# Windowed attention in front of an MLP: blocks of 128 keys by 64 queries of two heads, with block-diagonal queries in place of block-diagonal keys, another order of the transposed copies, and V shifted on the chip

## The chip, the cores and the metric

The kernel runs on one core of one Trainium2 chip. The metric is the device time in microseconds (us) of one execution, given as the median of several. The profiles are of single executions, and their span (first to last instruction) is some 2 us shorter than the time of the same run. TensorE is called PE below, its weight loads PEld, VectorE DVE, ScalarE ACT and GpSimd POOL, as the profile does.

A run is called slow when it is over 1.5% above the fastest of the same kernel.

## The reference

```python
# q, k, v: (8 batches, 8 heads, 576, 64) float32;  w_in (512, 2048), w_out (2048, 512)
scores = q @ k.T / 8                          # per batch and head
mask   = (rel >= 0) & (rel < 64)              # rel = query position - key position
attn   = softmax(where(mask, scores, -1e9))
x      = (attn @ v), heads side by side       # 4608 tokens x 512
h      = x @ w_in
out    = (h - tanh(h)) @ w_out                # 4608 x 512 float32
```

A query sees itself and the 63 keys before it. So 64 neighbouring queries need 127 keys, and 64 neighbouring keys serve 127 queries.

## The kernel before

Both kernels weave the attention of one pair of heads (a *cycle*) into four steps of the MLP. A step is one hp product of four matmuls, tanh and a subtraction, and four matmuls of yp for the chunk of 512 tokens before. There are nine chunks of 16 steps. In the profile's names, `tp` are the transposed queries and keys in PSUM, `qt` and `kt` (or `ktb`) their copies in SBUF, `sp` the scores, `pt` their exponentials, `ov` the product PV, `rc` and `xs` the normalisation, `tpx` and `xT` the transposed output, `th` the tanh, `gT` the subtraction and `ysb` the copy of yp out of PSUM. These are the parts that the change touches; the MLP is the same in both.

```python
kTb  = [const.tile([128, S, 2], BF16) ...]        # keys: column 2t+h holds head h's 64 channels, zero elsewhere
qT   = [const.tile([128, S + 64], BF16) ...]      # queries of both heads, one above the other
vaug = [const.tile([128, NP, NJ, 130], BF16) ...] # partition 2p+i: key p of head i; a ones column per head

def load_v(b):                                    # 128-byte pieces into every second partition
    for i in range(2):
        nc.gpsimd.dma_start(out=vaug[b % NV][i::2, :, :, 65 * i:65 * i + 64]..., in_=v[...])

def tr(g, which):                                 # rows -> channels on partitions
    ...                                           # 6 transposes of 96 rows into PSUM: tp[channel, e, p]; position = 6p + e
    if which == "q":
        nc.scalar.activation(qT[g % NR][:, 0:S].rearrange("c (p e) -> c e p", e=E6), tp, ACT.Copy)
    else:
        for i in range(2):
            nc.vector.tensor_copy(
                kt[64 * i:64 * i + 64, :, i].rearrange("c (p e) -> c e p", e=E6),
                tp[64 * i:64 * i + 64])

def scores(g, grp):                               # 3 matmuls: 64 keys of two heads x 128 queries, then exp into PT
    ...
def masking(g):                                   # PT *= mask, on VectorE
    ...
def pv(g, t0, t1):                                # up to 3 matmuls per 128 queries, added up in PSUM; then 1/sum on VectorE
    ...

    # the schedule of pair g; "early" is after hp of a step, "late" is after yp
    at(early, a, tr, g, "q");          at(late, a, tr, g, "k")
    at(early, a + 1, scores, g, 0);    at(early, a + 1, scores, g, 1);  at(late, a + 1, scores, g, 2)
    at(early, a + 2, masking, g)
    at(late, a + 2, pv, g, 0, 3);      at(late, a + 3, pv, g, 3, 5)
```

The PSUM tile holds e outermost and p innermost, and the SBUF tile wants position 6p + e. The kernel before walks along p. So it reads PSUM densely and writes one 2-byte element every 12 bytes (queries) or every 24 bytes (keys, where two heads alternate).

The softmax here doesn't subtract the row's maximum and nothing guards it: scores larger than these inputs give would overflow.

## Time and profile before

| | before |
|---|---|
| time, median of 4 runs | 642.86 us (642.23 to 643.35) |
| span of the profiled run, granted clock | 641.7 us, 0.837 |
| PE busy, DVE busy | 63%, 56% |
| one cycle (one pair, four steps) | 17.0 us; 20.8 where a batch's output is transposed |

The view is the table of stretches of the kernel before: start, chunk 0, the long stage and the plain MLP at the end. Its columns are the stretch, its length, busy time and count of PE, PEld, DVE, ACT and POOL, the granted clock, the share of the DMA engines and GB/s.

```profile
0.00:71.80 71.80, 19.95 (x177) 16.72 (x178) 45.68 (x54) 17.49 (x20) 30.61 (x45) 1.00 1.22 171
71.80:144.00 72.20, 41.04 (x223) 21.87 (x221) 41.56 (x50) 22.59 (x33) 8.61 (x10) 0.66 0.19 20
144.00:553.50 409.50, 264.92 (x1619) 135.89 (x1619) 240.45 (x281) 140.12 (x206) 41.45 (x48) 0.81 0.25 49
553.50:641.70 88.20, 79.88 (x387) 36.23 (x385) 28.51 (x47) 30.23 (x51) 0.00 (x0) 0.98 0.11 42
```

The long stage is two thirds of the time, with PE busy for 65% of it at 0.81 of the clock. (The trace's clock record of this kernel begins 81 us after the start of the span, and a mean counts what lies before it as full clock. So the 1.00 of the first row is no measurement, and the 0.66 of the second is a little too high: the first hp matmuls of chunk 0, before 81 us, follow each other every 427 ns, against 216 where the record says full clock.)

### The profile page before, as it was taken

The numbers are of one execution on the slowest core, as the hardware profiler recorded it, in microseconds if no ns is written. First come the engines' busy times: TensorE is split into PE (matmuls) and PEld (weight loads), VectorE is DVE, ScalarE is ACT, GpSimd is POOL, SyncE is SP. The second block draws the span as 40 slices with busy tenths as digits, with TensorE's granted clock in tenths as the row PEclk, the third lists the DMA queues.
The fourth block names the chain that finished last, engine by engine and source line by source line (L and its number), as shares of the span: only waits on it lengthen the run. The fifth ranks groups of instructions, "written<-read, shape, count | busy, mean of one in ns | idle before, by whom it ended". The sixth has DMA issues, their size and how long they took to land.

```text
span 641.7 us, 6133 instructions
## 1 busy us (share of the span) xinstructions
PE 405.8 (63%) x2400; PEld 210.7 (33%) x2400; DVE 356.2 (56%) x431; ACT 210.4 (33%) x309; POOL 80.7 (13%) x103
## 2 busy tenths in 40 slices
PE   0145555556667666656667766656666766699996
PEld 0134222233334333333333333333333333344442
DVE  3875556566654556566664555656665555544330
ACT  2142133333333233333333333333333333334431
POOL 3912100040103110031103110031111100000000
PEclk9999966668888777778888777777889777799999
DMA  9998900060118211161119111161111100000101
GB/s 198 177 199 113 129 1 0 1 38 0 54 53 89 56 53 55 53 37 55 53 54 90 54 54 53 54 41 50 54 54 54 53 17 17 16 34 33 51 33 66
DMA packets 59964, 37.62 MB, mean 59 GB/s; under 512 B 38944, under 2 KB 55328, under 8 KB 59936
## 3 DMA queue, kind: packets, MB, share of 16 engines
q0 software_dynamic: 41440, 8.91, 17.6%
q1 hardware_dynamic: 18496, 28.32, 15.6%
q8 instruction: 19, 0.31, 0.2%
q14 instruction: 9, 0.07, 0.0%
HBM read 36.70 MB, written 9.44 MB: 72 GB/s over the span
## 4 chain that ended last, share of the span: by engine, by line
PE 42%; DVE 24%; issue 6%; ACT 5%; POOL 1%; DMA 1%; SPq 0%; POOLq 0%; ACTq 0%
DVE ktb L157 18%; PE yp L226 17%; PE hp L212 16%; PE sp L165 4%; PE ov L185 3%; DVE gT L218 3%; ACT th L215 2%; DVE pt L171 2%; PE tp L151 2%; ACT qt L153 2%; ACT ysb L231 1%; PE tpx L196 1%; DMA qf<-in_q_dram 1%; POOL qb L77 1%; DVE xT L202 0%
## 5 line engine op out<-in xcount | busy, mean ns | idle before, releaser
L218 DVE TENSOR_TENSOR gT<-hp,th 128x512 bf16<-128x512 f32 x144 | 99.6, 692 | 189.4 <-ACT th L215 188.6
L212 PE MATMUL hp<-xT,w_in_sb 128*128 128x512 bf16 x576 | 179.9, 443 | 0.1
L157 DVE COPY ktb<-tp 64x576 bf16<-64x576 bf16 x64 | 171.7, 2684 | 13.1 <-PE tp L151 11.6
L226 PE MATMUL yp<-w_out_sb,gT 128*128 128x512 bf16 x576 | 167.5, 422 | 2.8 <-ACT ysb L231 2.8
L215 ACT ACTIVATE th<-hp 128x512 f32<-128x512 f32 x144 | 89.6, 622 | 192.6 <-PE hp L212 192.6
L165 PE MATMUL sp<-qt,ktb 128*128 128x128 bf16 x288 | 42.9, 309 | 164.5 <-DVE ktb L157 163.5
L167 ACT ACTIVATE pt<-sp 128x384 bf16<-128x384 f32 x96 | 44.0, 493 | 195.9 <-PE sp L165 195.9
L165 PEld LDWEIGHTS <-ktb 128*128 128x128 bf16 x288 | 30.0, 140 | 187.7 <-DVE ktb L157 176.0
L226 PEld LDWEIGHTS <-gT 128*128 128x128 bf16 x576 | 60.7, 109 | 75.3 <-issue 30.8
L212 PEld LDWEIGHTS <-w_in_sb 128*128 128x128 bf16 x576 | 58.7, 111 | 53.5 <-issue 20.7
L153 ACT ACTIVATE qt<-tp 128x576 bf16<-128x576 bf16 x32 | 66.9, 2089 | 21.2 <-PE tp L151 21.2
L185 PE MATMUL ov<-vaug,pt 128*128 128x130 bf16 x416 | 40.3, 244 | 40.8 <-DVE pt L171 37.1
L77 POOL CAST qb<-qf 96x768 bf16<-96x768 f32 x32 | 26.6, 831 | 207.5 <-DMA qf<-in_q_dram 192.9
L185 PEld LDWEIGHTS <-pt 128*128 128x128 bf16 x416 | 30.8, 109 | 65.4 <-DVE pt L171 52.5
L89 POOL DMA_DIRECT2D vaug<-in_v_dram x14 | 16.2, 1162 | 206.7 <-PE ov L185 206.7
L191 DVE TENSOR_TENSOR xs<-ov,rc 128x384 bf16<-128x384 f32 x64 | 31.4, 491 | 2.2
L189 DVE RECIPROCAL rc<-ov 128x6 f32<-128x6 f32 x64 | 11.8, 185 | 29.6 <-PE ov L185 29.6
L231 ACT ACTIVATE ysb<-yp 128x512 f32<-128x512 f32 x36 | 21.4, 593 | 17.5 <-PE yp L226 17.5
L77 POOL CAST kb<-kf 96x768 bf16<-96x768 f32 x32 | 26.5, 829 | 0.9 <-POOL qb L77 0.3
L202 DVE COPY xT<-tpx 128x512 bf16<-128x512 bf16 (+1 forms) x44 | 15.2, 369 | 19.2 <-PE tpx L196 19.2
L171 DVE TENSOR_TENSOR pt<-pt,mask 128x1152 bf16<-128x1152 bf16 x32 | 24.0, 749 | 0.2
L151 PE MATMUL tp<-ident,qb 96*128 96x96 bf16 x192 | 15.2, 222 | 14.0 <-POOL qb L77 7.4
(26 smaller groups left out, 95.9 us busy)
## 6 DMA issues: line engine op xcount, KB each, us to landing
qf<-in_q_dram SPq DMA_DIRECT2D x32, 288.0 KB, 3.4
kf<-in_k_dram SPq DMA_DIRECT2D x32, 288.0 KB, 3.8
out_dram<-ysb SPq DMA_DIRECT2D x36, 256.0 KB, 2.1
vaug<-in_v_dram POOLq DMA_DIRECT2D x14, 288.0 KB, 7.2
w_in_sb<-in_moe_w_in_dram POOLq DMA_DIRECT2D x4, 512.0 KB, 10.0
w_out_sb<-in_moe_w_out_dram POOLq DMA_DIRECT2D x4, 512.0 KB, 22.0
vaug<-in_v_dram POOLq DMA_DIRECT2D x8, 72.0 KB, 5.5
```

The lines of the kernel that those rows point to most:

```text
L77: nc.gpsimd.tensor_copy(t.rearrange("p e h d -> p h e d"), stage.pop((g, n)).rearrange("p h (e d) -> p h e d", d=D))
L153: nc.scalar.activation(qT[g % NR][:, 0:S].rearrange("c (p e) -> c e p", e=E6), tp, ACT.Copy)
L157: nc.vector.tensor_copy(kt[64 * i:64 * i + 64, :, i].rearrange("c (p e) -> c e p", e=E6), tp[64 * i:64 * i + 64])
L165: nc.tensor.matmul(sp[:, i, :], kTb[g % NR].rearrange("c t h -> c (t h)")[:, 128 * j:128 * j + 128], qT[g % NR][:, 64 * j:64 * j + 128], s ...
L167: nc.scalar.activation(PT[g % NR][:, 3 * grp:3 * grp + 3, 0:128], sp, ACT.Exp, scale=scale)
L171: nc.vector.tensor_tensor(p, p, mask.unsqueeze(1).to_broadcast([128, NJ, 128]), ALU.mult)
L185: nc.tensor.matmul(ov[:, t - t0, :], ptf[:, c0:c0 + 128], vaug[b % NV][:, pr, j, :], start=(i == 0), stop=(i == len(parts) - 1))
L191: nc.vector.tensor_tensor(xo, ovr[:, :, :, 0:64], rc[:, 0:n].to_broadcast([128, n, 2, 64]), ALU.mult)
L212: nc.tensor.matmul(hp, w_in_sb[:, ki, m * 128:(m + 1) * 128], chunk_tile(c)[:, ki, :], start=(ki == 0), stop=(ki == 3))
L215: nc.scalar.activation(th, hp, ACT.Tanh)
L218: nc.vector.tensor_tensor(gT[c][:, m, :], hp, th, ALU.subtract)
L226: nc.tensor.matmul(yps[c, s], gT[c][:, m, s * 128:(s + 1) * 128], w_out_sb[:, m, :], start=(m == 0), stop=(m == M - 1))
```

## The change

Its intent: lay a block out as 128 keys by 64 queries of two heads. Then the keys stay plain, the queries become block-diagonal (two copies of half a tile), one PV matmul of 128 keys serves a window of 64 queries of both heads, and nothing has to be added up in PSUM. The 128 keys are the window's own 64 and the 64 before; so V stands twice in SBUF, the second time moved on by one block of 64 keys, by a transfer on the chip (`shift_v`). The copies after the transposes now walk along the written side, so that the stepping is on the PSUM side. The core of the diff:

```diff
+    vw = [const.tile([128, NP, NJ, 129], BF16, ...)]      # partitions 64-127: keys of block j; 0-63: of block j-1
+    kT = [const.tile([128, 64 + S], BF16, ...)]
+    qT = [const.tile([128, NJ, 2, 64], BF16, ...)]
+    def load_v(b, p0=0, p1=NP):
+        for i in range(2):
+            nc.gpsimd.dma_start(out=vw[b % NV][64:128, p0:p1, :, 64 * i:64 * i + 64]..., in_=v[...])
+    def shift_v(b, p0=0, p1=NP):
+        w = vw[b % NV].rearrange("p r j c -> p r (j c)")
+        nc.sync.dma_start(out=w[0:64, p0:p1, 129:], in_=w[64:128, p0:p1, :(NJ - 1) * 129])
 ...
     def tr(g, which):
 ...
-            nc.scalar.activation(qT[g % NR][:, 0:S].rearrange("c (p e) -> c e p", e=E6), tp, ACT.Copy)
+            t = tp.rearrange("c e (j a) -> c j e a", a=8)
+            o = qT[g % NR].rearrange("c j h (e a) -> c j h e a", e=E)
+            nc.scalar.activation(o[0:64, :, 0], t[0:64], ACT.Copy)
+            nc.vector.tensor_copy(o[64:128, :, 1], t[64:128])
         else:
-            for i in range(2):
-                nc.vector.tensor_copy(
-                    kt[64 * i:64 * i + 64, :, i].rearrange("c (p e) -> c e p", e=E6),
-                    tp[64 * i:64 * i + 64])
+            nc.scalar.activation(kT[g % NR][:, 64:].rearrange("c (p e) -> c p e", e=E),
+                                 tp.rearrange("c e p -> c p e"), ACT.Copy)
 ...
     def pv(g, grp):
+        for i in range(3):
+            j = 3 * grp + i
+            nc.tensor.matmul(ov[:, i, :], PT[g % NR][:, j, :], vw[b % NV][:, pr, j, :], start=True, stop=True)
+        # one reciprocal and two multiplies (one per head) for each group of three windows
 ...
-        at(late, a + 2, pv, g, 0, 3)
-        at(late, a + 3, pv, g, 3, 5)
+        at(late, a + 2, pv, g, 0)
+        at(early, a + 3, pv, g, 1)
+        at(late, a + 3, pv, g, 2)
 ...
+    at(late, -8, load_v, 1)
+    at(late, -4, shift_v, 1)
+    for i in range(4):
+        at(late, -3 + i, load_w_out, i)
```

Cut are the memsets, the mask, the casts, the transposes of the output (now half a batch at a time), and the writes of the result, which put the rows of a window back into their order.

## The prediction

> **What bounds the kernel now.** I read the page first: no engine is full (PE 63%, VectorE 56% of the 641.7 us span), so a sum of busy time does not decide. The chain that ended last does: 18% of the span lies on one VectorE line, the copy that makes the block-diagonal keys.
>
> ```profile
> PE 42%; DVE 24%; issue 6%; ACT 5%; POOL 1%; DMA 1%; SPq 0%; POOLq 0%; ACTq 0%
> ...
> L157 DVE COPY ktb<-tp 64x576 bf16<-64x576 bf16 x64 | 171.7, 2684 | 13.1 <-PE tp L151 11.6
> ...
> L165 PE MATMUL sp<-qt,ktb 128*128 128x128 bf16 x288 | 42.9, 309 | 164.5 <-DVE ktb L157 163.5
> ```
>
> The third row says what it costs: TensorE stood 163.5 us before the score matmuls, all of it for that copy. It is 32 waits of 5.1 us, one for each pair of heads. Next, the chain in order of time in the middle of the run, over one such cycle (one pair of heads and four steps of the two MLP matmuls, hp and yp):
>
> ```profile
> 311.91 0.26 PE tp L151 x6
> 312.17 0.86 PE yp L226 x4
> 313.04 0.27 PE tp L151 x6
> 313.31 0.02 issue
> 313.33 2.69 DVE ktb L157
> 316.03 0.01 issue
> 316.04 2.69 DVE ktb L157
> 318.73 0.05 issue
> 318.78 0.82 PE sp L165 x6
> 319.60 1.71 PE yp L226 x4
> 321.31 0.32 PE sp L165 x3
> 321.63 1.72 PE hp L212 x4
> ```
>
> Two copies of 2.69 us stand between the transposes of the keys and the scores, and only one hp (0.86 us) lies beside them. The cycle repeats after 17.0 us (scores at 301.79, 318.78, 335.79). And the same yp of four matmuls takes 0.86 us before the wait and 1.71 after it. The table of short stretches (time, length, busy and count of PE, PEld, VectorE, ScalarE, POOL, then the granted clock) shows why:
>
> ```profile
> 309.78:313.19 3.41, 3.41 (x31) 1.99 (x30) 1.90 (x5) 1.84 (x3) 1.49 (x2) 1.00 0.00 0
> 313.19:316.60 3.41, 0.97 (x7) 0.23 (x3) 3.34 (x3) 1.77 (x2) 0.00 (x0) 0.97 0.00 0
> 316.60:320.02 3.42, 1.24 (x8) 0.92 (x9) 2.81 (x2) 0.70 (x2) 0.00 (x0) 0.50 0.00 0
> 320.02:323.43 3.41, 3.41 (x13) 1.41 (x11) 0.00 (x0) 1.21 (x4) 0.00 (x0) 0.53 0.00 0
> ```
>
> A stretch of 3.41 us with PE busy for only 0.97 is followed by two at half clock. So each wait is paid twice: 4.6 to 5.1 us idle and some 3 us of work at half speed.
>
> The hp matmuls give the stages: start until the first hp 71.8 us; then 27 cycles until 553.5 (17.0 us each, 20.8 where a batch's output is transposed into xT); then 88.2 us of plain MLP, where hp and yp follow each other every 0.86 us, at PE's speed.
>
> **What the Trainium skill says.** "TensorE: Matmul & The Clock Gate", Part 1: the clock is halved after a window of about 3.4 us with little activity and restored after a busy one. The trace agrees: over all stretches of 3.41 us, those at full clock with 0.8 to 1.2 us of PE work were followed by half clock, those with 1.96 or more stayed; none lies between. "SBUF — State Buffer", Specifications: SBUF has 16-byte lines, and each access that goes to a new line pays. It agrees: the keys' copy writes one 2-byte element every 24 bytes and takes 2684/576 = 4.7 ns an element, ScalarE's copy of the queries (every 12 bytes) 2089/576 = 3.6; copies that write dense (xT: 419 ns for 512, 283 for 256) take 0.53 and a fixed 147. "VectorE: DVE Perf Modes", The perf-mode tier table: a bf16 copy from PSUM may do two elements a cycle, tensor_tensor from PSUM one. It agrees (0.53 above; xs: 558 ns for 384, 424 for 256, so 1.05 ns and a fixed 156). "PSUM — Partial Sum Buffer", Specifications: 8-byte lines in PSUM. No row here shows what a stepped 2-byte read from PSUM costs.
>
> **Removed.** The two key copies, 2 x 2684 ns on VectorE per pair, and the 2089 ns query copy on ScalarE. Four PV matmuls per pair (13 become 9). Start: two memsets of 2.0 us and the ones columns.
>
> **Added per pair.** Keys: one ScalarE copy, dense writes, stepped reads. From exp (384: 493 ns), tanh (512: 622) and ysb (512: 593) I take 0.66 us for 576. Queries: half on ScalarE (0.66), then half on VectorE, which in the order of instructions waits for ScalarE's half; 147 + 576 x 0.53 = 0.45 us, or 0.76 at one element a cycle. Normalisation in three groups of three windows instead of two: three reciprocals of 0.16 and six multiplies of 64x192, 156 + 192 x 1.05 = 0.36 us each; 2.6 us against 1.35. Transposes: 16 of 72 columns for 12 of 96. Other additions: the shift of V (0.5 MB per batch, sync queue) and two output DMAs for one; both hidden, nine steps ahead of use or behind the end. VectorE saves 5.4 + 1.35 - 0.45 - 2.6 = 3.7 us per pair, but the gain is the wait.
>
> **One cycle after, at full clock.** PE: 8 x 0.86 for hp and yp, 16 transposes 0.6, 9 scores 0.5, 9 PV 0.5: 8.5 us. Latencies from the trace: hp's start to tanh 1.07, tanh 0.60, gT 0.69, 0.03 to 0.06 between engines. Now I lay the four steps out, zero at hp of step A:
> - A: hp to 0.86, transposes of q to 1.16, yp to 2.02, transposes of k to 2.32. ScalarE: tanh to 1.67, q half to 2.35, k to 3.2. VectorE: gT to 2.39, q half to 2.86.
> - B: hp to 3.18; scores at 3.26, a wait of **0.1** in place of 5.1; yp and the last scores to 4.63. ScalarE: tanh to 4.0, three exps to 5.35, ysb to 5.92.
> - C: hp to 5.49; yp needs its one PSUM buffer, which ysb frees at 5.92: wait **0.5**, to 6.84. Tanh after ysb to 6.52, gT to 7.24, mask 0.75 to 7.97; PV 1 waits **1.2** (the trace before has 1.2 there too), to 8.17.
> - D: hp to 9.03; the one ov buffer is free after reciprocal and two multiplies at 9.2: wait **0.2**; yp to 10.29. Now gT of D stands first on VectorE (to 10.56), then 0.9 us of normalisation: PV 3 waits **1.2**, to 11.67.
>
> So 8.5 + 3.2 = 11.7 us. Where half a batch is transposed (every second pair) 9 transposes (0.5) and waits for two tp buffers (0.8) are added: 13.0. Mean 12.3, against 17.95 (three of 17.0, one of 20.8).
>
> **The other stages.** Start: the two sparse copies go (5.4 us for each of four pairs), but all of V of batch 0 must land before the shift. The first V pair landed at 15.9 us here, with some 2.5 MB moved; I put the rest at 22, the shift at 25, then nine PV groups one after another on one buffer (PV at half clock 0.5, 0.9 on VectorE, about 1.5 each) and some 5 us of masks, transposes and scores: first hp at 44 (estimate, in place of 71.8). The four cycles of chunk 0 (the first 512 tokens, 16 steps) have no yp and too little PE work to be clocked up; the same layout at half clock gives 14.9 each, and 3 for xT: 63 us. Re-warming 3. Then 23 cycles of 12.3: 283. End: 86. Sum 44 + 63 + 3 + 283 + 86 = 479; I say **480 us**.
>
> **Rivals.** (1) The stepped PSUM read is as slow as the stepped write: the k copy takes 2.1 us, scores start 1.35 later, 27 x 1.35 = 36 us: 515. For it: the same access, other side. Against: the penalty is only shown for writes. (2) The one ov buffer becomes the bound, and the clock drops: the thinnest stretch, from B's end to PV 1, has about 1.8 us of matmuls and 0.3 of drain in 3.41, near the 1.96 that stayed at full clock. If it falls, about 3 us per cycle: 550. (3) V's load and shift come late, the sync queue, which serves them in order, holds back q and k: start near 60, 496. (4) The waits removed were hidden behind something else that takes their place in full, so nothing is gained: against it, PE does 8.5 us of work in 17.0 and no other engine has more than 9 in a cycle.
>
> **Range and chances.** (1) 25%, (2) 20%, (3) 20%; the other side is that waits overlap better than on paper (11.5 a cycle: 460). Range 445 to 530. The wait of 163.5 us is so plainly on the path that faster by over 2% gets 0.96, within 2% 0.02, slower 0.02 (the half clock throughout).
>
> **What would show it.** The wait of sp near zero; kt copy near 0.66 us (2 us: rival 1); new waits of ov for xs near 1.2 us once per pair and of yp for ysb near 0.5; granted clock near 1.0 from 110 us on (0.5 windows: rival 2); cycle 11.7 and 13.0; first hp at 44; last 88 us as before. The prediction is wrong if the dense writes are not fast, or if PE gets half its clock for these short waits.

## The result, and the profile after

| | before | after |
|---|---|---|
| time, median of 4 runs | 642.86 us (642.23 to 643.35) | 490.53 us (488.67 to 491.31) |
| ratio | 1 | 0.7627 (95%: 0.7604 to 0.765) |
| span, granted clock | 641.7 us, 0.837 | 488.4 us, 0.967 |

A ratio here and below is the mean time of one kernel's fast runs over that of the other's fast runs in the same rounds, so it is not quite the ratio of the medians quoted. The predicted 480 was 10.5 us too low; 490.53 lies within the range of 445 to 530.

The page of the changed kernel, first the rows on the keys (row by row: who copied what, busy time and mean ns of one, then PE's or ACT's idle time before it and what ended it):

```profile
L167 PE MATMUL sp<-qt,kt 128*128 128x128 bf16 x288 | 30.5, 241 | 4.7 <-ACT kt L160 2.4
L160 ACT ACTIVATE kt<-tp 128x576 bf16<-128x576 bf16 x32 | 20.8, 650 | 24.2 <-PE tp L153 24.2
```

The idle time before the scores is 4.7 us, of which 2.4 for the keys; before it was 164.5 and 163.5. The copy takes 650 ns. The stages of the changed kernel, with the columns as above:

```profile
0.00:57.60 57.60, 19.36 (x180) 14.59 (x181) 22.37 (x62) 14.71 (x26) 27.33 (x37) 1.00 2.05 153
57.60:125.30 67.70, 38.21 (x221) 20.21 (x220) 27.64 (x66) 19.30 (x37) 13.55 (x14) 0.77 1.17 93
125.30:401.00 275.70, 221.48 (x1624) 105.93 (x1623) 158.48 (x377) 120.51 (x233) 50.31 (x48) 1.00 0.87 83
401.00:488.40 87.40, 77.38 (x366) 34.62 (x365) 28.95 (x49) 29.02 (x49) 0.00 (x0) 0.99 0.13 42
```

Most of the gain lies in the third row: 409.5 us became 275.7, or 134 of the 153 us. The same 1,620 or so matmuls are in it, but PE is busy for 221 us instead of 265, because the clock is 1.00 instead of 0.81. DVE does 158 us instead of 240. Chunk 0 still runs for the most part at half clock: its 0.77 is too high, since the record of this kernel begins only at 81.0 us; from there to 125.3 us it is 0.65, and 33 of the 48 distances between the hp matmuls of one step are at the 427 ns of half clock. The start takes 57.6 us.

What took the place of the wait is seen in the chain, over the second half of one cycle in the long stage (start, length, what):

```profile
208.92 0.59 ACT ysb L229
209.51 0.50 ACT th L213
210.01 0.02 issue
210.03 0.69 DVE gT L216
210.73 0.67 DVE pt L173
211.40 0.05 issue
211.45 0.35 PE ov L180 x3
```

No key copy is on it any more. PE now waits for the mask (`pt`), which stands in DVE's order behind gT, which waits for tanh, which stands in ACT's order behind ysb, the copy of yp. The sums over the run, from the view of PE's waits (total us, how often, the longest):

```profile
PE ov L180 <- DVE xs L186: 41.8, 63, 2.0
PE ov L180 <- DVE pt L173: 29.3, 28, 2.1
PE ov L180 <- DMA vw<-vw: 25.0, 3, 10.8
```

The first two rows are inside the cycles: PV waits for the one `ov` buffer (freed by the normalisation, `xs`) and for the mask. The third is the shift of V, three times, in the start and chunk 0. The chain at the start:

```profile
20.21 36.33 DMA vw<-in_v_dram
...
56.59 14.80 DMA vw<-vw
...
71.43 0.38 PE ov L180 x2
```

The load of batch 1's V takes 36.3 us and its shift 14.8, and a PV stands behind them until 71.4 us, with the first hp at 57.6 and the second only at 71.6. What the first hp itself waited for is batch 0's V, in the timeline of PE (start, length, what, and in brackets the wait before it):

```profile
28.38 0.38 PE L180 MATMUL ov<-vw,pt 128*128 128x129 bf16 x2 [10.76 <-DMA vw<-vw]
...
38.77 0.38 PE L180 MATMUL ov<-vw,pt 128*128 128x129 bf16 x2 [4.62 <-DMA vw<-vw]
```

The load of pairs 1 to 3 of batch 0 landed at 26.3 us, and PV could go on only after their shift, 12.4 us later. Nine PV groups, transposes and scores then took the 18.8 us to the first hp. The page's section on queues shows the same V traffic from the side of the transfers. Before:

```profile
q0 software_dynamic: 41440, 8.91, 17.6%
```

After:

```profile
q0 software_dynamic: 41376, 8.91, 62.7%
```

As many packets and bytes take 62.7% of the engines' time instead of 17.6%: 0.176 x 641.7 x 16 / 41440 = 0.044 us a packet before, 0.627 x 488.4 x 16 / 41376 = 0.118 after. From the records of V's 36,864 packets of 128 bytes alone: mean 37.7 ns before, 118.2 after. These times overlap, and the delay of a load is smaller than their ratio: in the long stage the packets of one batch's V pass in some 8.3 us, against 5.3 before. Nor are the slow packets simply the misaligned half: 59% of the packets take over 60 ns (8% before), in the long stage nearly all of the second half of a load and a quarter of the first.

### The profile page after: what moved, and what is told of

Its sections match the earlier page's. It is cut to its first block, busy times and chain, and to the rows that moved or that the text cites. A ratio compares the mean times of both kernels' runs of the same rounds, so it can differ in the third digit from the quotient of the medians.

```text
span 488.4 us, 6341 instructions
## 1 busy us (share of the span) xinstructions
PE 356.4 (73%) x2384; PEld 175.4 (36%) x2384; DVE 237.4 (49%) x553; ACT 183.5 (38%) x342; POOL 91.2 (19%) x97
## 3 DMA queue, kind: packets, MB, share of 16 engines
q0 software_dynamic: 41376, 8.91, 62.7%
## 4 chain that ended last, share of the span: by engine, by line
PE 49%; DVE 20%; DMA 13%; ACT 12%; issue 4%; POOL 1%; SPq 1%; ACTq 0%; POOLq 0%
PE hp L210 23%; PE yp L224 15%; DVE gT L216 10%; ACT th L213 8%; DMA vw<-in_v_dram 7%; PE ov L180 4%; DVE xs L186 4%; DVE pt L173 4%; ACT ysb L229 3%; DMA vw<-vw 3%; PE sp L167 3%; PE tp L153 3%; DMA kf<-in_k_dram 3%; DVE xT L200 1%; PE tpx L192 1%
## 5 line engine op out<-in xcount | busy, mean ns | idle before, releaser
L210 PE MATMUL hp<-xT,w_in_sb 128*128 128x512 bf16 x576 | 157.5, 398 | 0.0
L224 PE MATMUL yp<-w_out_sb,gT 128*128 128x512 bf16 x576 | 145.9, 379 | 7.5 <-ACT ysb L229 7.5
L180 PE MATMUL ov<-vw,pt 128*128 128x129 bf16 x288 | 37.3, 242 | 100.7 <-DVE xs L186 41.8
L82 POOL CAST qb<-qf 72x1024 bf16<-72x1024 f32 x31 | 32.9, 1061 | 202.3 <-DMA qf<-in_q_dram 168.8
L186 DVE TENSOR_TENSOR xs<-ov,rc 64x192 bf16<-64x192 f32 x192 | 68.2, 355 | 4.6
L82 POOL CAST kb<-kf 72x1024 bf16<-72x1024 f32 x31 | 32.4, 1046 | 13.0 <-DMA kf<-in_k_dram 5.4
L167 PE MATMUL sp<-qt,kt 128*128 128x128 bf16 x288 | 30.5, 241 | 4.7 <-ACT kt L160 2.4
L91 POOL DMA_DIRECT2D vw<-in_v_dram x18 | 19.9, 1113 | 66.9 <-PE ov L180 66.2
L160 ACT ACTIVATE kt<-tp 128x576 bf16<-128x576 bf16 x32 | 20.8, 650 | 24.2 <-PE tp L153 24.2
L167 PEld LDWEIGHTS <-kt 128*128 128x128 bf16 x288 | 21.7, 108 | 22.4 <-ACT kt L160 12.7
L157 ACT ACTIVATE qt<-tp 64x576 bf16<-64x576 bf16 x32 | 20.3, 636 | 11.1 <-PE tp L153 11.1
## 6 DMA issues: line engine op xcount, KB each, us to landing
vw<-in_v_dram POOLq DMA_DIRECT2D x14, 288.0 KB, 10.8
vw<-in_v_dram POOLq DMA_DIRECT2D x2, 216.0 KB, 18.8
```

Of the source, the lines that this page charges most:

```text
L82: eng.tensor_copy(o, i)
L167: nc.tensor.matmul(sp[:, i, :], kT[g % NR][:, 64 * j:64 * j + 128], qT[g % NR][:, j].rearrange("c h t -> c (h t)"), start=True, stop=True)
L180: nc.tensor.matmul(ov[:, i, :], PT[g % NR][:, j, :], vw[b % NV][:, pr, j, :], start=True, stop=True)
L186: nc.vector.tensor_tensor(xs[b % 2][r, 3 * grp:3 * grp + 3, pr, :], ov[r, :, r], rc[r].to_broadcast([64, 3, 64]), ALU.mult)
L210: nc.tensor.matmul(hp, w_in_sb[:, ki, m * 128:(m + 1) * 128], chunk_tile(c)[:, ki, :], start=(ki == 0), stop=(ki == 3))
L224: nc.tensor.matmul(yps[c, s], gT[c][:, m, s * 128:(s + 1) * 128], w_out_sb[:, m, :], start=(m == 0), stop=(m == M - 1))
```

## The experiments

After the result I held this theory (A): the gain comes from the order of the copies, which takes away the stepped writes, the wait, and by that the half clock. The new layout has little to do with it. What was lost to the prediction lies at the start, in V's misaligned rows (258 bytes) and in the order of the loads. The rivals were that the layout itself brings the gain (fewer PV matmuls, less work on DVE), that the clock is a bystander, and that the slow V comes from the other traffic. In the texts A is mine, and each run names what else it is to tell apart. Each kernel was timed in three rounds; the runs of the kernel before in the same rounds had medians of 641.04 (e1 to e4), 642.22 (e5 to e8) and 642.46 (e9 to e11). All eleven gave correct results.

| run | made from | one change | median us | ratio to before (95%) |
|---|---|---|---|---|
| after | | the whole change | 490.53 | 0.7627 (0.7604–0.765) |
| e1 | before | order of the copies alone | 453.33 | 0.7065 (0.7045–0.7085) |
| e2 | before | 28 idle matmuls in the wait | 590.44 | 0.9193 (0.9158–0.9228) |
| e3 | after | keys written with a step again | 556.58 | 0.866 (0.8629–0.8691) |
| e4 | after | V's rows 260 bytes | 474.30 | 0.7385 (0.7365–0.7406) |
| e5 | after | V of batch 1 before the weights | 482.70 | 0.752 (0.7489–0.7552) |
| e6 | after | mask half a step earlier | 454.55 | 0.7074 (0.7051–0.7097) |
| e7 | e6 | PV groups one step apart | 431.35 | 0.666 (0.6604–0.6716) |
| e8 | e1 | mask earlier, half the keys on ACT | 420.90 | 0.6549 (0.6526–0.6573) |
| e9 | after | e4, e5 and e7 together | 415.10 | 0.6462 (0.6436–0.6488) |
| e10 | e1 | mask earlier, keys half a step earlier | 411.11 | 0.6405 (0.6379–0.6431) |
| e11 | e4 | head 1's V two bytes off | 487.27 | 0.7583 (0.7555–0.7611) |

The same by stages, from the profiles, cut at the subtraction gT of steps 0, 16 and 108 (so the long stage is 23 cycles):

| us | to the first gT | chunk 0 | long stage | rest | span |
|---|---|---|---|---|---|
| before | 74.4 | 72.2 | 409.5 | 85.7 | 641.7 |
| after | 60.2 | 66.9 | 274.4 | 87.0 | 488.4 |
| e1 | 53.7 | 44.3 | 267.0 | 85.7 | 450.8 |
| e4 | 49.1 | 62.3 | 274.3 | 87.0 | 472.7 |
| e5 | 62.5 | 56.1 | 274.4 | 87.1 | 480.0 |
| e6 | 60.5 | 55.8 | 250.4 | 86.0 | 452.6 |
| e9 | 54.4 | 38.4 | 233.3 | 85.7 | 411.8 |
| e10 | 51.3 | 36.1 | 236.3 | 84.7 | 408.5 |

### e1: the order of the copies alone, in the kernel before

```diff
-   nc.scalar.activation(qT[..][:, 0:S].rearrange("c (p e) -> c e p", e=E6), tp, ACT.Copy)
+   nc.scalar.activation(qT[..][:, 0:S].rearrange("c (p e) -> c p e", e=E6),
+                        tp.rearrange("c e p -> c p e"), ACT.Copy)
-   nc.vector.tensor_copy(kt[64*i:64*i+64, :, i].rearrange("c (p e) -> c e p", e=E6), tp[64*i:64*i+64])
+   nc.vector.tensor_copy(kt[64*i:64*i+64, :, i].rearrange("c (p e) -> c p e", e=E6),
+                         tp[64*i:64*i+64].rearrange("c e p -> c p e"))
```

The same elements go to the same places; only the order differs. The keys are still block-diagonal, so they are still written with a step, but of 4 bytes instead of 24.

> The kernel before, only the copies of q and k out of the transposes go through the elements in the order in which they are written (q dense, keys at every second element), reading PSUM with a step; layout, PV and V loads as before. Theory A (the order of the writes is nearly the whole gain of the long stage): the two key copies fall from 2684 ns to about 750 ns each, the wait of the scores from 5.1 us to about 1 us a cycle, the clock stays near 1.0, cycle 11.3 to 12.3 us, total 460 to 500 us. Rival B (the gain needs the new layout with one key copy on ScalarE and fewer PV matmuls): the wait stays over 3 us a cycle, total over 560 us.

Measured: 453.33 us, a ratio of 0.7065. Theory A holds, and more than that: the time is below the expected 460 to 500, and the order alone gains more than the whole change. The rows of e1's page that answer to the two shown of before:

```profile
L166 PE MATMUL sp<-qt,ktb 128*128 128x128 bf16 x288 | 29.7, 236 | 44.8 <-DVE ktb L158 43.3
...
L158 DVE COPY ktb<-tp 64x576 bf16<-64x576 bf16 x64 | 50.9, 795 | 4.8 <-PE tp L151 3.3
```

A key copy takes 795 ns instead of 2684. In the middle of the run the wait of the scores for the keys is 0.84 us a cycle; the rest of the 43.3 us falls in the start and chunk 0. The cycle is 11.1 us (13.5 in one of four), mean 11.61 over the long stage, against 11.93 in the changed kernel. So from e1's side the new layout, as it was scheduled, cost 37 us: 6.5 in the start, 22.6 in chunk 0, 7.4 in the long stage and some 1 at the end (table). In chunk 0, PE's busy time alone is 28.1 us in e1 and 38.1 in the changed kernel: of the distances between hp matmuls 6 of 42 are those of half clock in e1, 33 of 48 in the changed kernel. The rest is mainly the wait for V (e5).

### e2: work in the wait, in the kernel before

```diff
     def scores(g, grp):
         sp = ps_s.tile([128, 3, 128], F32, ...)
+        if grp == 0 and g >= NP:
+            for _ in range(28):
+                nc.tensor.matmul(sp.rearrange("p a b -> p (a b)"), w_in_sb[:, 0, 0:128],
+                                 w_in_sb[:, 0, 0:384], start=True, stop=True)
```

The 28 products are of no use and are overwritten by the scores. They fill the 5 us in which PE waited for the keys and take away nothing.

> The kernel before, with 28 matmuls of 384 columns, whose result is overwritten, put into TensorE's wait for the key copy (28 x 160 ns = 4.5 us at full clock). The wait keeps its length. Theory A (each wait is paid a second time in half clock): granted clock near 1.0 after the first cycles, what follows the wait takes 2.2 us less, cycle 17.0 to about 14.8 us, total 570 to 595 us, although there is more work. Rival B (the half clock is hidden or not caused by the idle time): total 640 us or more.

Measured: 590.44 us, a ratio of 0.9193, at a clock of 0.981. A cycle is 14.93 us instead of 17.0. The timeline of e2, with start and length:

```profile
255.28 4.71 PE L165 MATMUL sp<-w_in_sb 128*128 128x384 bf16 x28
...
260.25 1.03 PE L230 MATMUL yp<-w_out_sb,gT 128*128 128x512 bf16 x4
```

The yp behind the empty wait, in the same view of the kernel before:

```profile
319.39 1.91 PE L226 MATMUL yp<-w_out_sb,gT 128*128 128x512 bf16 x4
```

It takes 1.91 us there and 1.03 behind the filled wait. So of the two prices of the wait in the prediction, the second is shown by itself: the half clock is worth 2.07 us a cycle or 8% of the whole, in a kernel that does more work and waits as long.

### e3: the stepped keys alone, in the changed kernel

```diff
-   nc.scalar.activation(kT[..][:, 64:].rearrange("c (p e) -> c p e", e=E), tp.rearrange("c e p -> c p e"), ACT.Copy)
+   nc.scalar.activation(kT[..][:, 64:].rearrange("c (p e) -> c e p", e=E), tp, ACT.Copy)
```

> The changed kernel, only the key copy on ScalarE reads densely and writes with a step of 16 bytes. Theory A (stepped writes are what costs): the copy takes about 2.1 us in place of 0.65, the scores wait some 1.4 us a cycle, total 515 to 535 us. Rival B (reading with a step costs as much as writing with one): copy and total unchanged within 2%, 490 us.

Measured: 556.58 us (fast runs 553.0 to 556.76), a ratio of 0.866. The direction is that of A; the size is past the expected one. The page of e3 (its profiled run was slow: 565.6 us, clock 0.925):

```profile
L160 ACT ACTIVATE kt<-tp 128x576 bf16<-128x576 bf16 x32 | 87.0, 2718 | 24.0 <-PE tp L153 23.9
```

The copy takes 2718 ns, not the 2.1 us that I took from the queries' copy of before. The scores waited 62 us for it (at most 2.9 at a time), and the clock fell in many cycles. Why it is dearer shows when the copies are set side by side. A ScalarE copy has a fixed 181 ns (from exp, 384 elements in 490 ns, and ysb, 512 in 593), a VectorE copy 147.

| copy | bytes from one write to the next | ns | ns an element |
|---|---|---|---|
| DVE, keys of before | 24 | 2684 | (2684 − 147) / 576 = 4.40 |
| ACT, keys of e3 | 16 | 2718 | (2718 − 181) / 576 = 4.40 |
| ACT, queries of before | 12 | 2089 | (2089 − 181) / 576 = 3.31 |
| DVE, keys of e1 | 4 | 795 | (795 − 147) / 576 = 1.13 |
| ACT, keys of after | 2, PSUM read with a step | 650 | (650 − 181) / 576 = 0.81 |
| DVE, half of the queries of after | runs of 16 bytes | 461 | (461 − 147) / 576 = 0.55 |

In these copies a write that goes to a new 16-byte line costs 4.40 ns on both engines. At a step of 12 bytes three of four writes go to a new line, and 3/4 x 4.40 = 3.30 is what is measured; at 4 bytes it is one of four, 1.10 against 1.13. DVE's dense writes (0.55, one of eight) fit too; ACT's (0.81) are slower than that, at the pace of exp and ysb (0.80). As a general rule this is not shown: ysb itself writes 4-byte elements, four to a line, at 0.80 ns each, less than the 4.40/4 = 1.10 that the rule would ask. A run with a step of 8 bytes, where half should pay, was not made.

### e4: rows of V of 260 bytes in place of 258

```diff
-    vw = [const.tile([128, NP, NJ, 129], BF16, ...)]
+    vw = [const.tile([128, NP, NJ, 130], BF16, ...)]     # and the shift and the memset to match
-            nc.tensor.matmul(ov[:, i, :], PT[..][:, j, :], vw[..][:, pr, j, :], ...)
+            nc.tensor.matmul(ov[:, i, :], PT[..][:, j, :], vw[..][:, pr, j, 0:129], ...)
```

With rows of 258 bytes every second piece of 128 bytes begins 2 bytes off a multiple of 4; with 260 none does.

> The changed kernel, only the rows of V are 130 elements apart (260 bytes, as before) instead of 129 (258 bytes); partitions 64 to 127 and the shift stay. In the changed kernel a 128-byte packet of V takes a mean of 118 ns against 38 before. Theory A (packets at addresses off a multiple of 4 bytes are slow): packets back to some 40 ns, V of batch 1 lands 10 us or more earlier, first hp near 45 us, total 465 to 480 us. Rival B (64 neighbouring partitions are slower than every second of 128): packets stay near 118 ns, total within 1% of 490 us.

Measured: 474.30 us, a ratio of 0.7385: 16 us for one column that nobody reads. The chain at the start of e4:

```profile
19.23 25.46 DMA vw<-in_v_dram
...
44.74 10.95 DMA vw<-vw
```

A packet of V takes 43.4 ns instead of 118.2. Batch 1's V lands after 25.5 us instead of 36.3, the shift after 10.95 instead of 14.8, and the first hp comes at 46.9 instead of 57.6. For batch 0, the load has landed at 20.1 us instead of 26.3, and PV goes on at 27.5 instead of 38.8. The long stage is 274.3 us, as in the changed kernel: there the slow packets were hidden.

### e5: V of batch 1 ahead of the weights

```diff
     load_v(0, 1, NP)
+    load_v(1)
 ...
-    at(late, -8, load_v, 1)
-        at(late, -3 + i, load_w_out, i)
+        at(late, 2 + 2 * i, load_w_out, i)
```

> The changed kernel (V rows still 258 bytes), only the order of the first loads is other: V of batch 1 is issued right behind V of batch 0, ahead of w_in, and w_out four to ten steps later. In the changed kernel V of batch 1 takes 36 us to land (56.5) and its shift 15, and TensorE waits 9.6 us for it right after the first hp. Theory A (this load stands behind the weights): that wait goes, chunk 0 takes about 10 us less, total 475 to 483 us. Rival B (the slow V packets fill the queues whatever the order): the time comes back as a later first hp, total within 1% of 490 us.

Measured: 482.70 us, a ratio of 0.752. Chunk 0 is 10.8 us shorter, since the wait for batch 1's shift is gone; the start is 2.3 us longer, presumably since batch 0's V now shares the engines with batch 1's. A packet of V still takes 126.8 ns, and in the changed kernel's long stage, where no weights are loaded, 122; so it is not the weights that make them slow. The result lies in A's range of 475 to 483, at its upper edge: taken alone, the order is worth 8 us and the alignment 16.

### e6: the mask half a step earlier

```diff
-        at(early, a + 2, masking, g)
+        at(late, a + 1, masking, g)
```

> The changed kernel, only the masking is issued half a step earlier, ahead of the next hp and its gT instead of behind them. Theory A (PV 1 waits because the mask stands behind gT on VectorE): its wait of 0.86 us falls to about 0.1, cycle 11.3 to 10.3 to 10.5 us, 27 cycles of 0.9: total 462 to 470 us. Rival B (the wait moves to the next PV, which needs the one ov buffer): total within 1.5% of 490 us.

Measured: 454.55 us, a ratio of 0.7074, below the expected 462 to 470. The mask now stands ahead of the next gT in DVE's order. The wait that was 29.3 us in the changed kernel, in e6's view of PE's waits:

```profile
PE ov L180 <- DVE pt L173: 1.5, 3, 0.5
```

The long stage is 24 us shorter, 1.04 us a cycle, of which the wait was 0.86. Chunk 0 is 11 us shorter, of which 9 are the same matmuls at a higher clock: PE is busy there for 29.2 us instead of 38.1.

### e7: the PV groups one step apart

```diff
 # e6, and
-        at(early, a + 3, pv, g, 1)
-        at(late, a + 3, pv, g, 2)
+        at(late, a + 3, pv, g, 1)
+        at(early, a + 4, pv, g, 2)
```

> As the previous one, and the three PV groups one step apart instead of half a step. Theory A (three groups on one buffer, half a step apart, cost the wait of 0.88 us before PV 3): waits for xs near 0.3 us a cycle, cycle near 9.6 us, total 440 to 455 us. Rival B (pairs with xT wait instead for the late normalisation): no gain over the previous one, within 1% of it.

Measured: 431.35 us (425.23 to 433.3), a ratio of 0.666; below the expected 440 to 455. The wait of PV for the normalisation fell from 41.8 to 20.0 us. The cycle is 9.2 to 9.4 us (11 with a transposed output), against 11.3 and 12.6 in the changed kernel. (Two of its four runs, 432.26 and the profiled 433.3 us, count as slow against the fastest, so the ratio rests on 425.23 and 430.43. But all four have the same clock, 0.992 to 0.998, so this is spread and not a lower clock.)

### e8: e1 with the mask earlier and the keys halved between DVE and ACT

```diff
 # e1, masking at late a + 1 as in e6, and
-                nc.vector.tensor_copy(o, t)              # both heads
+                if i == 0:
+                    nc.scalar.activation(o, t, ACT.Copy)
+                else:
+                    nc.vector.tensor_copy(o, t)
```

> The kernel before with dense write order (453 us), masking half a step earlier, and one of the two key copies on ScalarE. If the waits left there (scores for keys 0.84 us, PV for mask 0.87 us a cycle) are as independent as they look, cycle 11.1 to 9.3 to 9.6 us, total 405 to 420 us. If they give way to the one ov or yp buffer, total over 430 us.

Measured: 420.90 us, a ratio of 0.6549; just outside the expected 405 to 420. (The profiled run was slow: 427.4 us, clock 0.947.) Halving did nothing for the wait: it is 0.84 us a cycle as in e1, for DVE's half began only when ACT's half of the same PSUM tile had ended. Its part of the expectation was a miss. The gain against e1 is put down to the mask, since PV no longer waits for it; e1 with the mask alone was not run.

### e9: the changed kernel mended

e4, e5 and e7 together, no other edit.

> The changed kernel with four mends together: V rows 260 bytes, V of batch 1 loaded ahead of w_in, mask half a step earlier, PV groups one step apart. Theory (start and long stage are separate terms and add up): 490.5 - 59 (mask and PV) - 16 (rows) - up to 8 (order) = 407 to 417 us. Rival (the start is bound by the same few loads whichever mend is made): order adds nothing to the rows, 415 to 425 us.

Measured: 415.10 us, a ratio of 0.6462, within the expectation, but at the edge of its rival's range too (415 to 425). The three gains measured alone are 16.2, 7.8 and 59.2 us, or 83; together they are 75.4, which is just the sum of e4's and e7's. So the mends of rows and of the schedule add up, and the order's 7.8 us is not found again on top of them: the run does not decide against the rival.

### e10: e1 with the mask and the keys earlier

```diff
 # e1, and
-        at(late, a, tr, g, "k")
+        at(early, a, tr, g, "k")
-        at(early, a + 2, masking, g)
+        at(late, a + 1, masking, g)
```

> The kernel before with dense write order (453 us), masking half a step earlier, and the key transposes issued ahead of yp, so that one more yp (0.86 us) lies beside the two key copies; both copies stay on VectorE. Theory (the split of the copies over two engines gained nothing because the second half waited for the first, and what is needed is more work beside them): wait of the scores for the keys 0.84 us to near 0, cycle 11.1 to 9.3 to 9.7 us, total 403 to 418 us. Rival (VectorE is late anyway, with gT): wait stays over 0.5 us, total 420 us or more.

Measured: 411.11 us (410.35 to 412.03), a ratio of 0.6405, clock 1.00. It is the fastest version, at 1% below e9 (their intervals against before just do not overlap). It is the old layout, with four statements changed. The cycle is 9.9 us, a little above the 9.3 to 9.7 that I expected, and the reason given for the gain was a miss. The wait of the scores for the keys did not go to zero, in the view of waits from 150 to 325 us:

```profile
PE sp L166 <- DVE ktb L158: 8.3, 12, 0.7
```

It is still 0.69 us in three of four cycles, against 0.84 in e1, as the rival had said: in DVE's order the copies stand behind gT. So of the 1.18 us by which the cycle is shorter than e1's, 0.86 is again PV's wait for the mask, which is gone.

### e11: is it the offset of two bytes?

```diff
 # e4 (rows of 260 bytes), and head 1 two bytes further on
-                out=vw[b % NV][64:128, p0:p1, :, 64 * i:64 * i + 64]...
+                out=vw[b % NV][64:128, p0:p1, :, 65 * i:65 * i + 64]...
```

The row keeps its 260 bytes; head 1's values begin at element 65, as they do in the kernel before, and the ones stand at 129; PV's product takes all 130 columns.

> V rows of 260 bytes as in e4 (packets 43 ns), but the second head's values start at element 65, so that all of its packets start 2 bytes off a multiple of 4, as they do in the kernel before (which has them on every second partition, at 38 ns). Theory A (a packet that starts off a multiple of 4 is slow on these 64 neighbouring partitions): mean of the V packets 75 ns or more, total 478 to 490 us. Rival B (the parity does not matter, but rows of 258 bytes do, on which the two loads of the two heads meet within a 4-byte word): packets near 43 ns, total near 474 us.

Measured: 487.27 us (fast runs 486.56 to 487.78), a ratio of 0.7583, 13 us more than e4. (The profiled run, 549.8 us, was slow at a clock of 0.753, so only its packets are used.) A packet of V takes 93.8 ns on average. So the offset of two bytes is enough; the length of the row is not what matters. But the kernel before has the same offset in half of its packets, and they take 37.7 ns. What is left are two differences, not tested apart: it writes every second one of all 128 partitions, while these write neighbouring ones, and only partitions 64 to 127. Those 64 partitions alone do not make packets slow (e4, 43.4 ns). Why either should matter is open.

## Why the prediction was right

That the time came within 2% of 480 is in part luck: the start and chunk 0 took 20 us more than predicted, counted to the first gT, and the long stage and the re-warming 12 less. Of the steps:

- **The wait removed** was right: 163.5 us became 2.4. (The 32 waits of 5.1 us are a mean: the first was 17.6, those of the long stage 4.4 to 4.6.) The keys' copy was put at 0.66 us and is 0.650; DVE's half of the queries at 0.45 and is 0.461. Rival 1, a slow stepped read of PSUM, falls: 0.81 ns an element.
- **Every wait is paid twice**: right, and shown by e2, where filling the wait without shortening it gives 8%.
- **The cycle** was put at 11.7 and 13.0, and is 11.31 and 12.57. The new waits are the ones named, at somewhat smaller sizes: in the cycle from 208 us on, 0.20 for ysb (0.5 predicted), 0.86 for the mask (1.2), 0.17 and 0.88 for the ov buffer (0.2 and 1.2). With 23 cycles the long stage is 274 us against the 283 predicted.
- **The clock** was right for the long stage (full from 125 us on; rival 2 falls there) and for chunk 0, which stays for the most part at half. The thinnest stretch of 3.41 us in the long stage, on the boundaries of the clock record, has 2.2 us of PE work, more than the 1.8 that I put on paper. The prediction's limits of 1.2 and 1.96 us belong to its own stretches, which lie 0.2 us behind those boundaries; on the boundaries, 1.39 us or less was followed by half clock, and 1.77 or more was not.
- **The start** is the step that failed. The prediction said "I put the rest at 22, the shift at 25" and so "first hp at 44"; it came at 57.6. Batch 0's V landed at 26.3, and the term that was mis-sized most is its shift: 12.4 us where the prediction had 3, so that PV went on at 38.8. The 18.8 us from there to the first hp are the 18.5 predicted. This is rival 3 nearly to the number (60), and by its first half, V's load and shift; the queries and keys of batch 0 had been issued before the shifts, so that the sync queue did not hold them back. A packet of V took 118 ns where the trace before had 38. e4 mends V's rows alone, brings PV forward to 27.5 and has its first hp at 46.9. In other stages too a shift takes some 8 us from its first packet to its last, not 3; there it is hidden.
- **Chunk 0** was put at 63 and is 66.9 from gT to gT. Its first cycle takes 23.5 us instead of 14.9, with the 9.6 us for batch 1's V in it (e5). The other three are cheaper than 14.9 on average.
- **The end** was put at 86 and is 87.

Added up from the predicted 479: 13.6 more for the start, 3.9 for chunk 0, 8.6 less for the long stage, 3 less for a re-warming that was not found as a term of its own, 1 more for the end, and the 2.6 from the first hp to the first gT that the sum left out. That is 488.5, the span; the time of a run is 2 us longer.

What the prediction did not see is where the gain comes from. It counted the removal of the copies as a part of the layout. e1 shows that the order of the elements within the copies gives all of it and 37 us more; the layout as scheduled gave those back. Rival 2's 550 us, with a chance of 20%, lay outside the range given. With both schedules mended the two layouts are nearly equal: 415 us (e9) and 411 (e10). And the waits that it named at 1.2 us each, it took as given. Moving three lines of the schedule gains 59 us (e7). “No other engine has more than 9” us of work in a cycle holds only after the change (VectorE 6.9); before, VectorE had 10.5 (240.45/23).

Open are two things: why misaligned packets are slow on the neighbouring partitions 64 to 127 and not on every second of all 128, and how much of chunk 0's half clock in the changed kernel is due to each of its waits. Of the 48 distances between hp matmuls there, 33 are those of half clock in the changed kernel, 30 in e5, 13 in e6, and 10 in e9, where several waits were taken away at once.

## What to carry to other kernels

When a copy must reorder, let it walk along the written side and step on the PSUM side; look at the bytes between two writes before a layout is changed. Where PE waits for a few us in each cycle, count the half clock behind the wait as well, and then look for the half step of the schedule that puts the waited-for instruction ahead of a long chain in its engine's order. Give rows that a transfer writes a pitch that keeps every piece on a multiple of 4 bytes.

## What the Trainium skill lacked or had wrong

- "SBUF — State Buffer", Specifications, speaks of a penalty for each access to a new 16-byte line without a size. The runs show 4.40 ns a write on VectorE and on ScalarE, 3.31 on average at a step of 12 bytes, and 1.13 in all at a step of 4.
- "PSUM — Partial Sum Buffer", Specifications, warns that any access that is not contiguous slows matmuls down. It does not say what such a read costs ScalarE or VectorE. On ScalarE no cost showed: 0.81 ns an element of 2 bytes with a step of 144 bytes between them. On VectorE it was 1.13 with a step of 192, twice the dense 0.53, but there the write had a step as well (e1), so the read's share is not known.
- "TensorE: Matmul & The Clock Gate", Part 1, doesn't say how much work in a window keeps the clock up. In the kernel before, on the boundaries of its clock record, 1.39 us or less of PE work in 3.41 was followed by half the clock, 1.77 or more was not. In the other runs stretches between 1.5 and 1.7 went both ways (e1: 1.65 kept the clock, 1.68 lost it). And idle matmuls pay (e2: a ratio of 0.9193).
- "DMA: Bandwidth & Descriptors", Specifications, marks transfers under 512 bytes as below line rate, and “How a descriptor splits into AXI transactions” there counts what a start off a multiple of 256 bytes costs; neither has anything on a start off a multiple of 4. Packets of 128 bytes took 118 ns where half of them began 2 bytes off a multiple of 4 on neighbouring partitions, 43 where none did (e4), and 38 with that offset on every second one of all 128 partitions (before).
